# Row maxima of attention scores: one transpose of six columns and three two-head ScalarE operations in place of three transposes and two operations

## Chip, cores and metric

The kernel runs on one core of one Trainium2 chip. The metric is device time in microseconds (us) for one execution of the program. Engines are named as the profile names them: PE (TensorE, matrix products and transposes), PEld (its weight loads), DVE (VectorE), ACT (ScalarE), POOL (GpSimd), SP (SyncE, which issues most DMAs).

## What is computed

The reference is a clustered attention followed by a mixture of experts. Attention has 4 batches, 8 heads, 768 positions and 64 channels. Each query and key is assigned to one of 16 centroids, and a query sees only keys of its own centroid:

```python
mask = q_assign[:, :, :, None] == k_assign[:, :, None, :]
scores = scale * np.matmul(q, k.transpose(0, 1, 3, 2))
scores = np.where(mask, scores, -1000000000.0)
scores = scores - np.max(scores, axis=-1, keepdims=True)
attn = np.exp(scores)
attn = attn / (np.sum(attn, axis=-1, keepdims=True) + 1e-09)
return np.matmul(attn, v).astype(np.float32)
```

The 3072 attention rows of 512 channels then pass one of 8 experts each (two layers, 512 to 1024 to 512, with a relu between them), if a skip score is positive:

```python
e_idx = np.argmax(logits, axis=1)
for e in range(E):
    mask = e_idx == e
    h = np.maximum(xc[mask] @ w1[e], 0.0)
    y[mask] = gate_w[mask, None] * (h @ w2[e])
out[do_compute] = xc + y
```

## The kernel before

The 32 heads are worked on as 16 pairs, numbered 0 to 15. A pair has 24 score steps: two halves of 384 queries (`hf`), six blocks of 128 keys (`kt`), two heads (`a`). One step (`score`) makes a 128x384 tile of transposed scores with two products (L604 and L605), ACT exponentiates it into a slot of the tile PT (L607), and POOL adds the slots up over the key blocks (L613, L619), which gives the denominators. Every six steps a burst of 12 products with v follows (`avs`, L630).

The row maximum is subtracted inside the product. The left operand of L604 holds, below 64 channels and 32 mask rows, rows of constants for each head (a tile of KB); the right operand (a tile of QM, one per head, both in the big tile D) holds the negated maxima of the queries there. So the maxima, which come out of DVE with queries along the partitions, have to be turned into rows:

- `smax` makes scores with queries along the partitions (L569) and DVE reduces them over keys (L571) into a tile M.
- `mneg` (L578, DVE) reduces M to one maximum for each query and head. For a half these are three blocks of 128 queries by two heads, written as columns 96 and 97 of three 128x128 blocks of a tile MX, one MX for each half.
- `mrows` turns each block on PE (L586, three transposes into one PSUM bank, block b at columns 128 b), so that rows 96 and 97 of the bank hold the maxima of the two heads. Two ACT operations (L591), one for each head, then write rows 96 and 97, negated, of QM.

Every instruction of attention is recorded by one planner, `steps`: a heap of tasks with due times in score steps (the table PLAN, with exceptions for pairs 0 to 3 in FIRST). `mrows` of a pair's first half is due 4.5 steps before its first score, and that of its second half 5.5 steps after it. PSUM tiles come from a ring of seven banks: `take` pops the bank that has been free longest, `give` appends one, both at the time when the planner records them. Other users of this ring, which the text below names, are the turned similarities to centroids (L514, read by `first_max` on DVE in L494 and L497, which then gives the bank back), the turned denominators (L678) and the turned attention output of the pair before (L729).

`operand_buffers` runs at the start, before the first pair. On POOL it fills the constant rows of three KB buffers for each head (L289 to L293, 12 fills) and clears the two MX tiles (L297). Behind these, POOL makes the low parts of pair 0's operands (L463, two operations), those of pair 1 (L431, two), clears rows of QM (L405), and then takes up its sums.

Of the kernel before, what the change touches and what calls it, by code (L numbers as in the profile page):

```python
# [13 lines left out]
F32 = mybir.dt.float32  # L14
# [4 lines left out]
AF = mybir.ActivationFunctionType  # L19
ALU = mybir.AluOpType  # L20
AX = mybir.AxisListType
PSUM = bass.MemoryType.PSUM

P = 128
H, S, D, NCL = 8, 768, 64, 16
HP = H // 2
HALF = S // 2
NB = HALF // P
KT = S // P
NS = 2 * 2 * KT  # L30
BIG = 2.0 ** 33

# [47 lines left out]
class Kernel:  # L80
# [167 lines left out]
    def buffers(self):  # L248

        D, both, last = self.D, self.both, self.nbatch * HP - 1  # L250
        assert last % 2 == 1 and last % 3 == 0
        part = lambda at, n, w: [D[:, at + w * j:at + w * (j + 1)] for j in range(n)]
        ops = [part(at, 4, S) for at in (13824, 0, 3072)]
        self.QM, self.KB = [o[:2] for o in ops], [o[2:] for o in ops]
        self.HI = part(6144, 2, S)
        self.QC = [part(at, 4, S) for at in (7680, 10752)]
        raw = both.tile([P, 2, 2, S], F32, name="raw", tag="raw")
        self.RAW = [raw[:, n] for n in range(2)]
        vt = both.tile([P, 2, KT, P], F32, name="vt", tag="vt")
        self.VT = [self.fix.tile([P, KT, P], F32, name="vt0"), vt[:, 0], vt[:, 1]]  # L260
        self.OT = [self.fix.tile([P, S], F32, name=f"oT{n}") for n in range(5)]

        w = part(0, 3, 1024) + [None] * 3 + [D[:, 6144:7168], D[:, 3072:4096]]
        w += part(4096, 2, 1024) + [D[:, 7168:8192], None] + part(8192, 2, 1024) + part(10752, 2, 1024)
        self.W = {"w1h": w[:4], "w1l": w[4:8], "w2h": w[8:12], "w2l": w[12:]}
        self.HT = [u.rearrange("p (f t) -> p f t", t=P) for u in part(13824, 2, 1024)]
        self.X1 = [u.rearrange("p (k t) -> p k t", t=P) for u in part(15872, 2, DM)]
        t = self.PT.rearrange("p n q -> p (n q)")
        self.HS, self.YE, self.XG0 = t[:, :FF], t[:, FF:FF + DM], t[:, FF + DM:FF + 2 * DM]
        self.XO = t[:OT, FF + 2 * DM:FF + 3 * DM]  # L270
# [9 lines left out]
    def operand_buffers(self):  # L280

        nc, fix, npair = self.nc, self.fix, self.npair
        for i in range(min(3, npair)):
            for a in range(2):
                kk = self.KB[i][a].bitcast(F32)

                lo = 64 if i else 96
                if a:
                    nc.gpsimd.memset(kk[96:98, :], 1.0)  # L289
                    nc.gpsimd.memset(kk[lo:97, :], 0.0)  # L290
                else:
                    nc.gpsimd.memset(kk[lo:98, :], 0.0)
                    nc.gpsimd.memset(kk[96:97, :], 1.0)  # L293

        self.MX = [fix.tile([P, NB, P], F32, name=f"MX{hf}") for hf in range(2)]
        for t in self.MX:
            nc.gpsimd.memset(t, 0.0)  # L297

        self.M = [fix.tile([P, KT, 2, 3], F32, name=f"M{n}") for n in range(2)]
        for t in self.M:  # L300
            nc.vector.memset(t[:, :, :, 2:], -BIG / 2)
        nc.vector.memset(self.PT[:, :, HALF:], GUARD / S)
# [24 lines left out]
    def tasks(self, i):  # L327
# [27 lines left out]
        for hf in range(2):  # L355
            add(p["mneg"][hf], self.mneg, hf)
            add(p["mrows"][hf][0], self.mrows, hf, *p["mrows"][hf][1:])
            for g in range(0, KT, GROUP):
                add(12 * hf + 2 * (g + GROUP) + p["av"], self.avs, hf, range(g, g + GROUP))
# [204 lines left out]
    def smax(self, i, n):  # L564
# [8 lines left out]
        if i == 0 and n in range(*WARM[:2]):  # L573
            self.keep_busy(1, WARM[2])

    def mneg(self, i, hf):

        self.nc.vector.tensor_reduce(out=self.MX[hf][:, :, 96:98], in_=self.st[i]["m"][:, hf * NB:(hf + 1) * NB],  # L578
                                     axis=AX.X, op=ALU.max)

    def mrows(self, i, hf, wait, step):

        c, nc = self.st[i], self.nc
        mp = self.take(("MX", i, hf), [P, HALF])
        for b in range(NB):
            nc.tensor.transpose(out=mp[:, b * P:(b + 1) * P], in_=self.MX[hf][:, b, :], identity=self.ident)  # L586
        yield wait
        for a in range(2):
            if a:
                yield step  # L590
            nc.scalar.activation(out=c["qm"][a][96:98, hf * HALF:(hf + 1) * HALF], in_=mp[96:98, :], func=AF.Copy,  # L591
                                 scale=-1.0)
        self.give(("MX", i, hf))

    def pt(self, i, s):
        return self.PT[:, (i * NS + s) % self.NPT, :]

    def score(self, i, s):

        c, nc = self.st[i], self.nc  # L600
        hf, kt, a = s // (2 * KT), s // 2 % KT, s % 2
        sl, ks = slice(hf * HALF, (hf + 1) * HALF), slice(kt * P, (kt + 1) * P)
        ps = self.take("ps", [P, HALF])
        nc.tensor.matmul(ps, lhsT=c["kb"][a][0:98, ks], rhs=c["qm"][a][0:98, sl], start=True, stop=False)  # L604
        nc.tensor.matmul(ps, lhsT=c["kc"][a][:, ks], rhs=c["qc"][a][:, sl], start=False, stop=True)  # L605
        pt = self.pt(i, s)[:, :HALF]
        nc.scalar.activation(out=pt, in_=ps, func=AF.Exp, scale=D ** -0.5)  # L607
# [888 lines left out]
```

## Time and profile before

| | |
|---|---|
| median of 3 runs | 662.63 us (661.48 to 662.72) |
| the profiled execution, its own time | 662.12 us |
| its span, first to last instruction | 660.4 us |
| mean granted clock of PE | 0.989 |
| PE busy | 639.8 us, 97% of the span |
| DVE busy | 505.6 us, 77% |
| ACT busy | 417.3 us, 63% |
| POOL busy | 359.9 us, 54% |

The span is what the profile covers; 1.72 us of the execution's own time lie around it. Attention takes the first 440 us or so, the experts the rest. A busy share is an average over stages with different limits, so each stage has to be looked at by itself.

### The profile page before, as it was taken

What the parts mean: (1) busy time and instruction counts of PE and PEld (TensorE: products, weight loads), DVE (VectorE), ACT (ScalarE), POOL (GpSimd) and SP (SyncE); (2) the same over time, 40 slices, a digit from 0 to 9 for tenths busy, and PEclk for the clock granted to TensorE, in tenths of its full rate; (3) what the DMA queues carried; (4) which work ended last, traced back from release to release, by engine and by line L of the source; (5) the groups of instructions that cost most, each with busy time, mean ns of one, the idle gap of its engine ahead of it and who ended that gap; (6) DMA issues with size and microseconds to landing.
All of it is one profiled execution on the core that took longest, in us unless ns stands there. A gap on an engine that the chain in (4) does not pass through costs nothing.

```text
span 660.4 us, 12489 instructions
## 1 busy us (share of the span) xinstructions
PE 639.8 (97%) x4019; PEld 475.9 (72%) x4019; DVE 505.6 (77%) x1031; ACT 417.3 (63%) x935; POOL 359.9 (54%) x384
## 2 busy tenths in 40 slices
PE   7899999999999999999999999799999999999994
PEld 3667776776767767767767767455798898899893
DVE  7877787688988869998769899786689867666721
ACT  7467778677777777767777778454365454544620
POOL 8876777857758867668677777440331321121101
PEclk9899999999999999999999999799999999999998
DMA  7388647866786466555754652140386758566620
GB/s 216 108 198 223 157 140 197 224 184 171 200 224 175 124 168 163 165 137 158 202 145 119 156 136 82 45 151 25 128 283 222 258 189 276 184 199 226 200 77 33
DMA packets 54323, 110.12 MB, mean 167 GB/s; under 512 B 8599, under 2 KB 22807, under 8 KB 54256
## 3 DMA queue, kind: packets, MB, share of 16 engines
q1 hardware_dynamic: 51232, 101.92, 53.7%
q0 software_dynamic: 2624, 7.18, 3.1%
q8 instruction: 33, 0.54, 0.3%
q14 instruction: 34, 0.28, 0.2%
q10 hardware_dynamic: 400, 0.20, 0.1%
HBM read 60.93 MB, written 10.55 MB: 108 GB/s over the span
## 4 chain that ended last, share of the span: by engine, by line
PE 79%; DVE 8%; issue 6%; DMA 5%; ACT 0%; POOL 0%; POOLq 0%; DVEq 0%
PE ps L630 20%; PE ps L604 11%; PE ps L569 10%; PE ps L605 9%; DMA out<-yo,idw 3%; DVE M L571 3%; PE ph L1030 3%; PE ph L1029 3%; PE ph L1028 3%; PE py L1029 2%; PE py L1028 2%; PE py L1030 2%; PE ps L729 2%; PE ps L586 2%; PE ps L480 2%
## 5 line engine op out<-in xcount | busy, mean ns | idle before, releaser
L619 POOL TENSOR_TENSOR acc<-acc,PT 128x384 f32<-128x384 f32 x246 | 241.6, 1010 | 56.5 <-ACT PT L607 56.1
L607 ACT ACTIVATE PT<-ps 128x384 f32<-128x384 f32 x384 | 184.2, 492 | 94.7 <-PE ps L605 77.8
L571 DVE TENSOR_REDUCE M<-ps 128x1 f32<-128x384 f32 x384 | 200.3, 553 | 47.5 <-PE ps L569 46.5
L630 PE MATMUL ps<-PT,vt 128*64 128x385 f32 x768 | 140.2, 500 | 0.1
L604 PE MATMUL ps<-D 98*128 98x384 f32 x384 | 135.5, 353 | 4.1 <-DVE M L571 3.5
L569 PE MATMUL ps<-D 96*128 96x384 f32 x384 | 135.6, 359 | 0.8 <-ACT D L549 0.7
L605 PE MATMUL ps<-D 128*128 128x384 f32 x384 | 131.0, 341 | 0.0
L630 PEld LDWEIGHTS ps<-PT,vt 128*64 128x64 f32 x768 | 49.8, 137 | 57.8 <-issue 52.9
L604 PEld LDWEIGHTS ps<-D 98*128 98x128 f32 x384 | 73.4, 191 | 24.9 <-issue 19.0
L613 POOL TENSOR_TENSOR acc<-PT 128x384 f32<-128x384 f32 x64 | 54.3, 868 | 67.7 <-ACT PT L607 36.1
L569 PEld LDWEIGHTS ps<-D 96*128 96x128 f32 x384 | 73.7, 193 | 20.4 <-ACT x L751 7.2
L1186 POOL DMA_INDIRECT out<-yo,idw x15 | 20.3, 1350 | 114.0 <-DVE yo L1062 103.8
L605 PEld LDWEIGHTS ps<-D 128*128 128x128 f32 x384 | 73.6, 192 | 0.0
L1314 ACT ACTIVATE hh<-ph 128x256 fp32r<-128x256 f32 x56 | 21.4, 383 | 46.4 <-PE ph L1030 46.4
L1315 DVE SCALAR_TENSOR_TENSOR hl<-ph,hh 128x256 fp32r<-128x256 f32 x56 | 23.6, 422 | 33.6 <-ACT hh L1314 33.4
L1286 ACT ACTIVATE D<-wraw 128x1024 fp32r<-128x1024 f32 (+1 forms) x45 | 44.1, 1002 | 6.2 <-PE py L1030 4.7
L1028 PE MATMUL ph<-x2l,D 128*128 128x256 f32 x168 | 47.7, 284 | 0.0
L1029 PE MATMUL ph<-x2h,D 128*128 128x256 f32 x168 | 47.6, 283 | 0.0
L1028 PE MATMUL py<-D,hh 128*128 128x512 f32 x112 | 45.0, 402 | 0.0
L751 ACT ACTIVATE x<-ps,rs 128x64 f32<-128x64 f32 x162 | 36.1, 322 | 10.1 <-DVE rs L683 9.1
L1287 DVE TENSOR_TENSOR D<-wraw,D 128x1024 fp32r<-128x1024 f32 (+1 forms) x29 | 34.3, 1183 | 6.2 <-ACT D L1286 5.4
L431 DVE TENSOR_TENSOR raw<-raw,D 128x768 fp32r<-128x768 f32 x28 | 38.3, 1367 | 0.0
(311 smaller groups left out, 1068.9 us busy)
## 6 DMA issues: line engine op xcount, KB each, us to landing
wraw<-w SPq DMA_DIRECT2D x72, 512.0 KB, 4.9
D<-D SPq DMA_DIRECT2D x124, 192.0 KB, 3.4
raw<-qk SPq DMA_DIRECT2D x16, 768.0 KB, 5.6
D<-raw SPq DMA_DIRECT2D x60, 192.0 KB, 4.1
vt<-v SPq DMA_DIRECT2D x16, 384.0 KB, 4.4
out<-x SPq DMA_DIRECT2D x31, 192.0 KB, 3.3
D<-mk SPq DMA_DIRECT2D x120, 24.0 KB, 1.9
out<-yo,idw POOLq DMA_INDIRECT x15, 4.5
```

What stands on the lines that cost most here:

```text
L431: eng.tensor_tensor(out=lo.bitcast(F32R), in0=lo, in1=c[f"hi{t}"].bitcast(F32), op=ALU.subtract)
L569: nc.tensor.matmul(sm, lhsT=c["qm"][a][0:96, j * P:(j + 1) * P], rhs=c["kb"][a][0:96, hf * HALF:(hf + 1) * HALF], start=True, stop=True)
L571: nc.vector.tensor_reduce(out=c["m"][:, j, a, hf:hf + 1], in_=sm, axis=AX.X, op=ALU.max)
L604: nc.tensor.matmul(ps, lhsT=c["kb"][a][0:98, ks], rhs=c["qm"][a][0:98, sl], start=True, stop=False)
L605: nc.tensor.matmul(ps, lhsT=c["kc"][a][:, ks], rhs=c["qc"][a][:, sl], start=False, stop=True)
L607: nc.scalar.activation(out=pt, in_=ps, func=AF.Exp, scale=D ** -0.5)
L613: nc.gpsimd.tensor_tensor(out=acc, in0=self.pt(i, s - 2)[:, :HALF], in1=pt, op=ALU.add)
L619: (nc.vector if dve else nc.gpsimd).tensor_tensor(out=acc, in0=acc, in1=pt, op=ALU.add)
L630: nc.tensor.matmul(av[a * D:(a + 1) * D, :], lhsT=c["vt"][:, kt, a * D:(a + 1) * D], rhs=self.pt(i, hf * 2 * KT + kt * 2 + a), start=(kt = ...
L1028: mm(ps, lhsT=ah, rhs=bl, start=first, stop=False)
L1029: mm(ps, lhsT=ah, rhs=bh, start=False, stop=False)
L1286: nc.scalar.activation(out=h[:, cs], in_=r[:, cs], func=AF.Copy)
```

## The change

In all pairs but the first and the last (14 pairs, 28 halves), `mneg` writes the six maxima of a query row (two heads by three blocks) into six neighbouring columns, 96 to 101, of one 128x128 tile. One transpose turns them, so that the bank's rows 96 to 101 hold three blocks of head 0 and three of head 1, all in the same 128 columns. Three ACT operations follow, one for each block b of 128 queries: each reads the six rows, multiplies every row with its own entry of a small constant tile `blocks` (1 in the two rows of block b, 0 in the four others), and writes the result, six rows by 128 columns, for both heads at once. So QM has six maximum rows, of which two are not zero in any column, and KB has six constant rows, -1 in the three rows of its own head and 0 in the others; L604 contracts over 102 rows where it had 98. The bank is given back at the time of the first ACT operation, 0.05 steps earlier than before.

The first and the last pair (`apart`) keep three transposes and two ACT operations, with six rows each, from two tiles MX3 of their own. At the start POOL has 16 fills of constant rows and clears four tiles, and DVE makes `blocks`.

```diff
-                lo = 64 if i else 96
-                if a:
-                    nc.gpsimd.memset(kk[96:98, :], 1.0)
-                    nc.gpsimd.memset(kk[lo:97, :], 0.0)
-                else:
-                    nc.gpsimd.memset(kk[lo:98, :], 0.0)
-                    nc.gpsimd.memset(kk[96:97, :], 1.0)
-
-        self.MX = [fix.tile([P, NB, P], F32, name=f"MX{hf}") for hf in range(2)]
-        for t in self.MX:
+                nc.gpsimd.memset(kk[96:MR, :], -1.0 if a else 0.0)
+                nc.gpsimd.memset(kk[96:96 + NB, :], 0.0 if a else -1.0)
+                if i:
+                    nc.gpsimd.memset(kk[64:96, :], 0.0)
+
+        self.MX = [fix.tile([P, P], F32, name=f"MX{hf}") for hf in range(2)]
+        self.MX3 = [fix.tile([P, NB * (P + 1)], F32, name=f"MX3{hf}") for hf in range(2)]
+        for t in self.MX3 + self.MX:
             nc.gpsimd.memset(t, 0.0)
...
+    def apart(self, i):
+        return i in (0, self.npair - 1)
+
     def mneg(self, i, hf):
 
-        self.nc.vector.tensor_reduce(out=self.MX[hf][:, :, 96:98], in_=self.st[i]["m"][:, hf * NB:(hf + 1) * NB],
-                                     axis=AX.X, op=ALU.max)
+        if self.apart(i):
+            mx = self.MX3[hf].rearrange("p (b c) -> p b c", b=NB)[:, :, 96:MR:NB]
+        else:
+            mx = self.MX[hf][:, 96:MR].rearrange("p (a b) -> p b a", a=2)
+        self.nc.vector.tensor_reduce(out=mx, in_=self.st[i]["m"][:, hf * NB:(hf + 1) * NB], axis=AX.X, op=ALU.max)
...
-        for b in range(NB):
-            nc.tensor.transpose(out=mp[:, b * P:(b + 1) * P], in_=self.MX[hf][:, b, :], identity=self.ident)
+        for b in range(NB if apart else 1):
+            nc.tensor.transpose(out=mp[:, b * P:(b + 1) * P],
+                                in_=self.MX3[hf][:, b * P:(b + 1) * P] if apart else self.MX[hf], identity=self.ident)
         yield wait
-        for a in range(2):
-            if a:
-                yield step
-            nc.scalar.activation(out=c["qm"][a][96:98, hf * HALF:(hf + 1) * HALF], in_=mp[96:98, :], func=AF.Copy,
-                                 scale=-1.0)
+        if apart:
+            for a in range(2):
+                if a:
+                    yield step
+                nc.scalar.activation(out=c["qm"][a][96:MR, n0:n0 + HALF], in_=mp[96:MR, :], func=AF.Copy)
+        else:
+            rows = self.QM2[i % 3][96:MR]
+            for b in range(NB):
+                nc.scalar.activation(out=rows[:, :, n0 + b * P:n0 + (b + 1) * P],
+                                     in_=mp[96:MR, :P].unsqueeze(1).to_broadcast([MR - 96, 2, P]), func=AF.Copy,
+                                     scale=self.blocks[96:MR, b:b + 1])
         self.give(("MX", i, hf))
...
-        nc.tensor.matmul(ps, lhsT=c["kb"][a][0:98, ks], rhs=c["qm"][a][0:98, sl], start=True, stop=False)
+        nc.tensor.matmul(ps, lhsT=c["kb"][a][:MR, ks], rhs=c["qm"][a][:MR, sl], start=True, stop=False)
```

Three places show what this does to the order of instructions. In these rows a bank of the ring is ps0_81 to ps6_87, ident_101 is the identity, and "waits" names the engines whose semaphores an instruction waits for. Line numbers of the changed kernel are its own (L586 has become L595, L514 L516, L678 L694, L729 L745, L630 L646, L569 L571).

The first place is PE at the second half of pair 3. Before, the maxima (L586), the turned similarities (L514), the turned denominators (L678) and the turned output of the pair before (L729):

```order
L586 MATMUL ps6_87<-ident_101,MX1_196 128x128 [waits DVE_49,Activation_49]
L586 MATMUL ps6_87<-ident_101,MX1_196 128x128 x2
L514 MATMUL ps4_85<-ident_101,ss_1197 128x128 [waits DVE_49,Activation_49]
L514 MATMUL ps4_85<-ident_101,ss_1197 128x128 x2
...
L678 MATMUL ps3_84<-ident_101,sr_1204 128x128 [waits Activation_49]
L678 MATMUL ps3_84<-ident_101,sr_1204 128x128 x2
L729 MATMUL ps4_85<-ident_101,oT2_96 128x128 [waits DVE_49]
L729 MATMUL ps4_85<-ident_101,oT2_96 128x128 x2
L630 MATMUL ps7_88<-PT_65,vt0_93 64x385 x6
L569 MATMUL ps6_87<-D_64 128x384 [waits Activation_49]
```

The same place in the changed kernel:

```order
L595 MATMUL ps3_84<-ident_101,MX1_202 128x128 [waits DVE_49,Activation_49]
L516 MATMUL ps4_85<-ident_101,ss_1202 128x128 [waits DVE_49,Activation_49]
L516 MATMUL ps4_85<-ident_101,ss_1202 128x128 x2
...
L694 MATMUL ps2_83<-ident_101,sr_1209 128x128 [waits Activation_49]
L694 MATMUL ps2_83<-ident_101,sr_1209 128x128 x2
L745 MATMUL ps3_84<-ident_101,oT2_96 128x128 [waits Activation_49]
L745 MATMUL ps3_84<-ident_101,oT2_96 128x128 x2
L646 MATMUL ps7_88<-PT_65,vt0_93 64x385 [waits DVE_49]
L646 MATMUL ps7_88<-PT_65,vt0_93 64x385 x5
L571 MATMUL ps4_85<-D_64 128x384 [waits DVE_49]
```

Two transposes are gone, and the banks have changed places: the turned output took the bank of the similarities (ps4_85, which DVE gives back) and now takes that of the maxima (ps3_84, which ACT gives back), and the next L569 the other way round.

The second place is ACT at the same half of pair 3: the denominators (L669), the maxima and two exponentials (L607). Before:

```order
L487 ACTIVATE ss<-ps_83 128x384 [waits PE_49]
L669 ACTIVATE sr<-ps_81 128x384 [waits DVE_49,PE_49]
L591 ACTIVATE D<-ps_87 2x384 [waits DVE_49,PE_49]
L591 ACTIVATE D<-ps_87 2x384
L607 ACTIVATE PT<-ps_86 128x384 [waits PE_49,Pool_49]
L607 ACTIVATE PT<-ps_83 128x384 [waits PE_49,Pool_49]
```

In the changed kernel:

```order
L489 ACTIVATE ss<-ps_87 128x384 [waits PE_49]
L685 ACTIVATE sr<-ps_81 128x384 [waits DVE_49,PE_49]
L606 ACTIVATE D<-ps_83,blocks 6x2x128 [waits PE_49]
L606 ACTIVATE D<-ps_83,blocks 6x2x128 x2
L623 ACTIVATE PT<-ps_86 128x384 [waits PE_49,Pool_49]
L623 ACTIVATE PT<-ps_87 128x384 [waits PE_49,Pool_49]
```

The two operations have become three, at the same place in ACT's queue, and the exponentials stand behind them as before.

The third place is POOL at the start, from the fills for pair 2's buffers on. Before:

```order
L292 MEMSET D 34x768
L293 MEMSET D 1x768 [waits Pool_49]
L289 MEMSET D 2x768
L290 MEMSET D 33x768 [waits Pool_49]
L297 MEMSET MX_195 128x384 [waits Pool_49]
L297 MEMSET MX_196 128x384
L463 TENSOR_TENSOR D<-raw,D 64x768 [waits DMAHW5_49,DMAHW1_49,DVE_49]
L463 TENSOR_TENSOR D<-raw,D 64x768 [waits DMAHW6_49,Pool_49]
L431 TENSOR_TENSOR raw<-raw,D 128x768 [waits PE_49,DMAHW2_49,Activation_49,Pool_49]
L431 TENSOR_TENSOR raw<-raw,D 128x768 [waits PE_49,Activation_49]
```

In the changed kernel:

```order
L291 MEMSET D 6x768
L292 MEMSET D 3x768 [waits Pool_49]
L294 MEMSET D 32x768
L299 MEMSET MX_203 128x387 [waits Pool_49]
L299 MEMSET MX_204 128x387
L299 MEMSET MX_201 128x128
L299 MEMSET MX_202 128x128
L465 TENSOR_TENSOR D<-raw,D 64x768 [waits DMAHW5_49,DMAHW1_49,DVE_49]
L465 TENSOR_TENSOR D<-raw,D 64x768 [waits DMAHW6_49,Pool_49]
L433 TENSOR_TENSOR raw<-raw,D 128x768 [waits PE_49,DMAHW2_49,Activation_49,Pool_49]
L433 TENSOR_TENSOR raw<-raw,D 128x768 [waits PE_49,Activation_49]
```

Four more fills of constant rows (of which the last three rows of 16 are shown) and two more cleared tiles stand ahead of the low parts of pairs 0 and 1.

## Rows read from the trace of the kernel before

**Rows 1.** The page: part 1, and the chain that ended last, by engine (part 4).
```profile
PE 639.8 (97%) x4019; PEld 475.9 (72%) x4019; DVE 505.6 (77%) x1031; ACT 417.3 (63%) x935; POOL 359.9 (54%) x384
...
PE 79%; DVE 8%; issue 6%; DMA 5%; ACT 0%; POOL 0%; POOLq 0%; DVEq 0%
```

**Rows 2.** Busy us by window: start:end, length, PE, PEld, DVE, ACT, POOL, PEclk, DMA, GB/s.
```profile
22.00:24.00 2.00, 1.98 (x9) 1.58 (x8) 1.91 (x5) 1.22 (x3) 1.92 (x4) 0.50 0.04 8
100.00:125.00 25.00, 25.00 (x155) 17.55 (x154) 18.31 (x36) 18.93 (x47) 18.87 (x20) 1.00 0.72 199
```

**Rows 3.** PE's waits: line, who was waited for, us in total, times, longest us.
```profile
PE ps L604 <- DVE M L571: 3.5, 1, 3.5
...
PE ps L729 <- DVE eqc L497: 0.6, 2, 0.3
```

**Rows 4.** Timeline of PE, second half of pair 3: start us, us, line, op.
```profile
106.01 0.55 PE L586 MATMUL ps<-ident,MX 128*128 128x128 f32 x3
...
108.12 0.55 PE L729 MATMUL ps<-ident,oT 128*128 128x128 f32 x3
```

**Rows 5.** Timeline of PE, first half of pair 4, in a wide and a narrow window.
```profile
119.64 0.34 PE L569 MATMUL ps<-D 96*128 96x384 f32 x1
119.82 0.49 PE L586 MATMUL ps<-ident,MX 128*128 128x128 f32 x3
120.24 0.55 PE L630 MATMUL ps<-PT,vt 128*64 128x385 f32 x2
...
119.82 0.27 PE L586 MATMUL ps<-ident,MX 128*128 128x128 f32 x1
```

**Rows 6.** Timeline of PE where no transpose stands between L569 and L630.
```profile
40.05 0.33 PE L569 MATMUL ps<-D 96*128 96x384 f32 x1
40.45 0.87 PE L630 MATMUL ps<-PT,vt 128*64 128x385 f32 x4
```

**Rows 7.** Timeline of ACT: the maxima, and operations with a scale in a tile.
```profile
14.37 1.02 ACT L549 ACTIVATE D<-ps,sel 32x384 fp32r<-32x384 f32 x2
...
106.74 0.86 ACT L591 ACTIVATE D<-ps 2x384 fp32r<-2x384 f32 x2
...
109.19 1.33 ACT L751 ACTIVATE x<-ps,rs 128x64 f32<-128x64 f32 x6 [0.65 <-DVE rs L683]
```

**Rows 8.** Timeline of POOL at the start.
```profile
3.00 0.73 POOL L292 MEMSET D<- 2x768 f32 x1
...
12.20 0.78 POOL L297 MEMSET MX<- 128x384 f32 x2
13.41 3.71 POOL L463 TENSOR_TENSOR D<-raw,D 64x768 fp32r<-64x768 f32 x2 [0.43 <-DVE D L463]
17.20 3.57 POOL L431 TENSOR_TENSOR raw<-raw,D 128x768 fp32r<-128x768 f32 x2
```

**Rows 9.** Timeline of PE and DVE at the first score and pair 1's centroids.
```profile
20.52 0.45 PE L604 MATMUL ps<-D 98*128 98x384 f32 x1 [0.57 <-ACT D L591]
...
20.43 0.75 DVE L502 TENSOR_TENSOR eqc<-eqc,wts 128x384 f32<-128x384 f32 x1
21.81 0.56 DVE L507 TENSOR_TENSOR oh<-wts,mwc 128x384 bf16<-128x384 f32 x1
...
22.42 0.24 PEld L527 LDWEIGHTS <-oh 128*128 128x128 bf16 x3 [0.53 <-DVE oh L507]
```

**Rows 10.** Timeline of DVE and POOL where both work from SBUF.
```profile
9.63 0.56 DVE L502 TENSOR_TENSOR eqc<-eqc,wts 128x384 f32<-128x384 f32 x1
...
42.43 1.22 DVE L502 TENSOR_TENSOR eqc<-eqc,wts 128x384 f32<-128x384 f32 x1
...
410.61 6.75 DVE L989 TENSOR_TENSOR cc<-ohd,ecode 128x48 f32<-128x48 bf16 x1
...
39.86 8.53 POOL L619 TENSOR_TENSOR acc<-acc,PT 128x384 f32<-128x384 f32 x8
...
410.13 7.16 POOL L619 TENSOR_TENSOR acc<-acc,PT 128x384 f32<-128x384 f32 x8
```

More of the change, by code (lines that the diff above doesn't have):

```diff
@@ L29 @@
 KT = S // P
+MR = 96 + 2 * NB
 NS = 2 * 2 * KT
@@ L253, in buffers @@
         ops = [part(at, 4, S) for at in (13824, 0, 3072)]
+        self.QM2 = [D[:, at:at + 2 * S].rearrange("p (a s) -> p a s", a=2) for at in (13824, 0, 3072)]
         self.QM, self.KB = [o[:2] for o in ops], [o[2:] for o in ops]
@@ L282, in operand_buffers @@
         nc, fix, npair = self.nc, self.fix, self.npair
+        self.blocks = fix.tile([P, NB], F32, name="blocks")
+        nc.vector.tensor_tensor(out=self.blocks, in0=self.ident[:, 96:96 + NB], in1=self.ident[:, 96 + NB:MR], op=ALU.add)
         for i in range(min(3, npair)):
@@ L574, in smax @@
             self.keep_busy(1, WARM[2])
+    def apart(self, i):
+        return i in (0, self.npair - 1)
     def mneg(self, i, hf):
-        self.nc.vector.tensor_reduce(out=self.MX[hf][:, :, 96:98], in_=self.st[i]["m"][:, hf * NB:(hf + 1) * NB],
-                                     axis=AX.X, op=ALU.max)
+        if self.apart(i):
[3 more added lines that the diff above has]
+        self.nc.vector.tensor_reduce(out=mx, in_=self.st[i]["m"][:, hf * NB:(hf + 1) * NB], axis=AX.X, op=ALU.max)
     def mrows(self, i, hf, wait, step):
         c, nc = self.st[i], self.nc
+        n0, apart = hf * HALF, self.apart(i)
         mp = self.take(("MX", i, hf), [P, HALF])
-        for b in range(NB):
-            nc.tensor.transpose(out=mp[:, b * P:(b + 1) * P], in_=self.MX[hf][:, b, :], identity=self.ident)
+        for b in range(NB if apart else 1):
+            nc.tensor.transpose(out=mp[:, b * P:(b + 1) * P],
+                                in_=self.MX3[hf][:, b * P:(b + 1) * P] if apart else self.MX[hf], identity=self.ident)
         yield wait
-        for a in range(2):
-            if a:
-                yield step
-            nc.scalar.activation(out=c["qm"][a][96:98, hf * HALF:(hf + 1) * HALF], in_=mp[96:98, :], func=AF.Copy,
-                                 scale=-1.0)
+        if apart:
[9 more added lines that the diff above has]
+                                     scale=self.blocks[96:MR, b:b + 1])
         self.give(("MX", i, hf))
```

## The prediction, made before the changed kernel was run

> **What bounds the kernel now.** I read the page first. PE is busy for 97% of the span, and the chain of work that ended last runs through PE for 79% of it [rows 1]. That is an average, so the next view is the table of busy time by window: in a stretch of pairs 3 and 4 PE is busy for 25.00 of 25 us at a granted clock of 1.00, while DVE (18.3) and ACT (18.9) have six us left [rows 2]. The list of PE's waits then has only one of weight inside attention, 3.5 us for one DVE reduction near the end, and two of 0.3 us each for L497 [rows 3]. So between the start and about 400 us PE's own instructions set the pace, and a PE instruction that is taken out there is worth the time until the next one can start.
>
> **What is removed.** 14 pairs times 2 halves times 2 transposes: 56 of PE's instructions. One is drawn 0.27 us long, but they overlap: in the narrow window one takes 0.27, in the wide one three take 0.49, so they start (0.49 - 0.27) / 2 = 0.11 us apart [rows 5]. Two fewer are worth 0.22 us, where the next instruction follows at once. That holds at a second half, where another three transposes (L514) come next. At a first half L630 comes next, and there I check it against a place without transposes: from L569 to L630 it takes 0.40 us with nothing between [rows 6] and 0.60 with three transposes [rows 5], so no more than 0.20 can be won. The term is 14 x 0.22 + 14 x 0.20 = 5.9 us. It can't be much more; it is less where PE then waits for something else.
>
> **What ACT gains.** Two operations on 2x384 take 0.86 us together; three on 6x2x128, 256 elements in a row and each with its scale read from a tile, take their place. No row shows this shape. The nearest from below is L751, 64 elements with a scale from a tile, 1.33 / 6 = 0.22 us each; from above L549, 384 elements with such a scale, 1.02 / 2 = 0.51 [rows 7]. So three cost between 0.67 and 1.53 us. By the number of elements, 0.22 + 0.29 x 192/320 = 0.40 each and 1.18 for the three, which I take: 0.32 us more in each half, 9 us in all on an engine with a quarter of its time left. Who waits for it? Behind them stand two exponentials, and behind those ACT is idle for 0.65 us before L751 [rows 7]; the first scores that read the maxima are four steps away by their due times. That covers 0.3 us.
>
> What is not covered is the bank. At the second half of a pair the turned output of the pair before, L729, used to take the bank that L497 on DVE gives back; now it takes the bank of the maxima, free when the third ACT operation ends. L729 stands at 108.12, 1.38 us after the ACT operations start at 106.74 [rows 4, 7]. With the transposes gone PE is there 0.22 earlier, after 1.16 us, and ACT needs 1.18 and a few hundredths for the signal: a wait of about 0.05. Nine of the second halves have this distance, within 0.06 us: 0.4 us in all. At the lower bound the wait is nothing, at the upper one 1.53 - 1.16 = 0.37, 3.3 us in all. In exchange the two waits for L497 go: 0.6 us won [rows 3].
>
> Here the Trainium skill speaks against the change. "ScalarE: Activation LUTs", section "What ACT_TABLE_LOAD costs", prices an operation at 186 ns plus 0.833 ns an element, 93 ns more for a scale read from a tile, with about 93 ns overlap between neighbours; as an estimate from that page three would take 1.29 us, and the sum would come out about 1 us higher. The trace agrees on the cost of the scale only in part: L549's pair lies above L591's by 0.08 us for each operation [rows 7].
>
> **What moves at the start.** POOL makes 12 fills and two cleared tiles from 3.00 to 12.98 before it is ready for L463, which starts at 13.41 and waits for DVE [rows 8]. The fills start (12.20 - 3.00) / 12 = 0.77 us apart, whatever their number of rows. Now there are 16, so the tiles start at about 3.00 + 12.3 = 15.3 at that pitch, or 14.7 if the fills without a wait of their own go closer; with 0.8 for the two larger tiles and 0.3 for the two smaller (a third of 0.39 each, rounded up), L463 starts at about 16.0 and ends at 19.7, some 2.5 us late. Its first reader, the second head's first score, comes behind the first L604 at 20.52 [rows 9], so that is hidden. L431 is next: it ran from 17.20 to 20.77 [rows 8] and would run from 19.7 to 23.3.
>
> That puts L431 on top of two DVE operations which read two operands from SBUF, L502 at 20.43 and L507 at 21.81; PE's L527 waits for L507 [rows 9]. Such operations get longer beside POOL's sums: L502 takes 0.56 us beside POOL's fills and 1.22 in the middle of eight POOL sums [rows 10]. So I let each wait for the POOL operation that is running. L431's two operations of 1.8 us end at about 21.5 and, after L502 has been let in, at 23.7. L502 then ends at 21.9, L505 follows, L507 waits from 22.5 to 23.7 and ends at 24.15, where it ended at 22.37: 1.8 us. PE waits behind L527 and works at half clock there (0.50, the 1.2 GHz level, [rows 2]) without a gap until the bursts begin, so 1.8 us stay. The bounds: nothing, if DVE gets its turn first, and 2.4 us if DVE has to wait for both of L431's operations.
>
> "SBUF — State Buffer" of the Trainium skill, section "Who interferes with whom", has the same: a DVE instruction with two SBUF inputs blocks against a POOL instruction that reads SBUF, and not against one that only writes. The trace shows it, 1.22 against 0.56 us [rows 10].
>
> The other edits cost nothing. `blocks` is one small DVE operation at about 6 us, where DVE next waits for PE; if it didn't, it would be some 0.1 us. The four longer fills cost what the shorter ones do. L604 over 102 rows instead of 98: L605 over 128 runs at the same pace. DVE's L578 writes as many elements. The DMA of pair 2's input, which waits for L463, goes out 2.5 us later, and its reader, the similarities of pair 2, is due five score steps behind the first score; the mask rows' DMAs wait for L405 behind L431, but also for the mask that follows L527, so they shift with it.
>
> **The sum,** against the profiled execution's own time: 662.12 - 5.9 (transposes) + 0.4 (bank) - 0.6 (waits for L497) + 1.8 (start) = 657.8 us. That execution lies 0.5 us below the median and inside the three runs' spread, so I leave the sum where it is: **657.8 us**.
>
> **Rivals.**
>
> 1. The start costs nothing: L431 leaves the gaps that DVE needs, or POOL is ready earlier. For it: L463 had 0.43 us in hand at the start of its run [rows 8]. Against: the fills' pitch is steady. 662.1 - 6.1 = 656.0 us.
> 2. ACT is at the upper bound, and L729 waits 0.37 us at each of nine pairs: 657.8 + 2.9 = 660.7. For it: no row has this shape, which writes two places from one. Against: it moves a third less for each operation than L549.
> 3. Slower than before: a DVE operation is caught behind a whole run of POOL sums. It happens once already: L989, 48 elements a row, takes 6.75 us, until the POOL run from 410.13 to 417.29 ends [rows 10], and PE then waits 3.5 us. By the rule of one instruction it would be 1 us. If one more operation on which PE waits is caught so, 657.8 + 6.7 = 664.5; it decides from 4.3 us on, that is, five sums of 0.9 us. For it: the change shifts PE and ACT against each other by half a us in every pair. Against: elsewhere in these rows one add was the longest wait.
> 4. The mirror of it: L989 falls outside the run, PE's 3.5 us wait goes: 654.3. As the order there is the same on all engines, I give it little.
> 5. The change takes nothing off PE's path: PE waits for others as long as it is early (L630 for exponentials, L569 for banks). Then only the start is left: 662.1 + 1.8 = 663.9. Against it stands a PE that is busy for 25.00 of 25 us.
>
> The same SBUF page says, in its section "SBUF: two separate sides", that the one who starts first holds the port for one whole instruction; by that, L989 should have waited for one sum, and the trace does not agree.
>
> **How the numbers follow.** Forecast 0.52 (its own range 656.6 to 659.2), rival 1 0.22, rival 2 0.08, rival 3 0.06, rival 4 0.07, rival 5 0.05. A measurement of this kernel can tell about 0.2%, 1.3 us, from no change: faster is below 661.3, slower above 664.0. Faster: the forecast, 1, 4 and half of 2 (the upper bound with a late start ends near 661), 0.85. Slower: 3 and part of 5, 0.08. The rest, 0.07, is no change. The range reaches from 655.2 to 661.2: it takes in rivals 1 and 2 and leaves out 3, 4 and 5, 0.18.
>
> **What would show it.** In the profile after: 40 transposes for the maxima (28, and 12 in the first and the last pair) where there were 96; one transpose of 0.27 us where three took 0.49; three ACT operations in 1.1 to 1.3 us; L729 (now L745) with small waits for ACT; L463 and L431 on POOL 2.5 us later, L507 longer or later, and L527 near 24.2. The bursts of L630 should come some 0.4 us earlier for each pair gone by, less what the start costs. It would be wrong if PE showed new waits for banks of some tenths in every pair, if PE's half clock at the start lasted longer with the wait, or if the DVE operation near 410 were gone or had a twin.

## The result, and the profile after

The changed kernel takes 653.13 us (median of 6 runs, 652.87 to 654.12); beside it the kernel before took 661.92 (6 runs, 659.60 to 662.72). The ratio is 0.9877, 95% interval 0.9857 to 0.9897: 8.8 us faster. Forecast were 657.8 us, in a range from 655.2 to 661.2. The direction was right and the time fell below the range.

The page of the changed kernel: its span, part 1, and the chain that ended last by engine (part 4).

```profile
span 651.5 us, 12396 instructions
...
PE 632.2 (97%) x3963; PEld 468.3 (72%) x3963; DVE 507.7 (78%) x1032; ACT 426.6 (65%) x963; POOL 364.1 (56%) x390
...
PE 75%; DMA 8%; DVE 8%; issue 7%; POOL 0%; ACT 0%; POOLq 0%; SPq 0%; DVEq 0%
```

Against [rows 1], PE has 56 instructions less, the two transposes in 28 halves, and ACT 28 more, one in each of these halves. PE is 7.6 us less busy, and the span is 8.9 us shorter. Where the rest comes from these sums don't say. For that I line up the two traces by the exponentials on ACT (L607, now L623), which come in the same order in both, and read the start of the first one of a half. Three points cut the span into four stretches:

| | to pair 0, step 12 | to pair 14, step 12 | to pair 15, step 12 | to the end | span |
|---|---|---|---|---|---|
| before | 33.98 | 369.83 | 32.20 | 224.39 | 660.4 |
| changed | 36.62 | 364.53 | 25.59 | 224.76 | 651.5 |
| difference | +2.64 | -5.30 | -6.61 | +0.37 | -8.9 |

So the shorter pairs gave 5.30 us and the start took 2.64. Together that is 2.7 us of gain. The other 6.6 us come out of one stretch near 410 us, in which the numbers of transposes and of ACT operations are those of before.

The start, on POOL (start us, us, line, operation):

```profile
14.60 0.73 POOL L294 MEMSET D<- 32x768 f32 x1
15.39 1.08 POOL L299 MEMSET MX<- 128x387 f32 x4
16.55 3.68 POOL L465 TENSOR_TENSOR D<-raw,D 64x768 fp32r<-64x768 f32 x2
20.31 3.90 POOL L433 TENSOR_TENSOR raw<-raw,D 128x768 fp32r<-128x768 f32 x2
```

on DVE, which works beside it:

```profile
20.40 2.15 DVE L504 TENSOR_TENSOR eqc<-eqc,wts 128x384 f32<-128x384 f32 x1
22.58 0.55 DVE L507 TENSOR_REDUCE mwc<-eqc 128x24 f32<-128x384 f32 x1
23.17 1.45 DVE L509 TENSOR_TENSOR oh<-wts,mwc 128x384 bf16<-128x384 f32 x1
```

and PE, which waits for it:

```profile
24.68 0.50 PE L529 MATMUL ps<-ident_bf,oh 128*128 128x128 bf16 x3 [2.12 <-DVE oh L509]
```

Against [rows 8, 9]: POOL's low parts stand 3.1 us later, the two DVE operations with two operands in SBUF fall on L433 and take 2.15 and 1.45 us where they took 0.75 and 0.56, and PE's L529 starts 2.26 us later. Behind it PE works at half clock, as these windows have it (start:end, length, busy us of PE, PEld, DVE, ACT and POOL, PEclk, DMA, GB/s):

```profile
24.00:26.00 2.00, 1.32 (x6) 1.32 (x7) 1.91 (x4) 0.67 (x1) 1.94 (x4) 0.50 0.04 11
26.00:28.00 2.00, 2.00 (x8) 2.00 (x8) 1.34 (x4) 0.93 (x2) 1.92 (x4) 0.50 0.09 22
```

In the pairs, the maxima on ACT and the turned output on PE at the second half of pair 3:

```profile
108.47 1.19 ACT L606 ACTIVATE D<-ps,blocks 6x256 fp32r<-6x256 f32 x3
```

```profile
107.74 0.33 PE L595 MATMUL ps<-ident,MX 128*128 128x128 f32 x1
...
109.71 0.55 PE L745 MATMUL ps<-ident,oT 128*128 128x128 f32 x3
```

The three operations take 1.19 us, and L745 starts 0.05 us behind their end. The group of L606 names who waited for it (its count, ns of one as min, median and max, and then us and times):

```profile
L606 ACT ACTIVATE D<-ps,blocks x84: 451/452/469, 45.5 to 395.2; 6x256 fp32r<-6x256 f32 x84
...
  PEld ps L745: 1.3, 8
```

Near 410 us, DVE and POOL:

```profile
407.93 3.20 DVE L1005 TENSOR_TENSOR cc<-ohd,ecode 128x48 f32<-128x48 bf16 x1
411.17 0.20 DVE L1008 TENSOR_REDUCE c<-cc 128x6 f32<-128x48 f32 x1
```

```profile
407.45 7.19 POOL L635 TENSOR_TENSOR acc<-acc,PT 128x384 f32<-128x384 f32 x8
```

and the windows around it, with the same columns:

```profile
409.00:412.00 3.00, 3.00 (x19) 2.19 (x13) 2.97 (x4) 1.99 (x6) 3.00 (x4) 1.00 0.00 0
412.00:415.00 3.00, 3.00 (x19) 2.06 (x21) 3.00 (x7) 2.75 (x5) 2.65 (x4) 1.00 0.01 3
415.00:418.00 3.00, 3.00 (x23) 1.95 (x23) 1.74 (x7) 2.29 (x7) 1.19 (x2) 1.00 0.23 72
418.00:421.00 3.00, 3.00 (x26) 1.49 (x19) 2.92 (x4) 2.16 (x6) 1.45 (x2) 1.00 0.42 168
```

This is the operation that took 6.75 us [rows 10], in front of the reductions on which PE waited 3.5 us [rows 3]. It meets the same run of eight sums, begins 0.48 us behind the start of that run's first sum as before, and ends after 3.20 us, 0.07 us behind the end of the fourth sum, while the run goes on to 414.64. PE has no wait here, and its granted clock stays at 1.00.

### The profile page after: what moved, and what is told of

The parts are those of the page before. It is cut to its first block, busy times and chain, and to the rows that moved or that the text cites. A ratio compares the mean times of both kernels' runs of the same rounds, so it can differ in the third digit from the quotient of the medians.

```text
span 651.5 us, 12396 instructions
## 1 busy us (share of the span) xinstructions
PE 632.2 (97%) x3963; PEld 468.3 (72%) x3963; DVE 507.7 (78%) x1032; ACT 426.6 (65%) x963; POOL 364.1 (56%) x390
## 4 chain that ended last, share of the span: by engine, by line
PE 75%; DMA 8%; DVE 8%; issue 7%; POOL 0%; ACT 0%; POOLq 0%; SPq 0%; DVEq 0%
PE ps L646 20%; PE ps L620 11%; PE ps L571 10%; PE ps L621 10%; DMA out<-yo,idw 5%; DVE M L573 3%; PE ph L1045 2%; PE ph L1044 2%; PE ph L1046 2%; PE py L1045 2%; PE py L1044 2%; PE ps L745 2%; PE py L1046 2%; PE ps L482 2%; PE ps L682 1%
## 5 line engine op out<-in xcount | busy, mean ns | idle before, releaser
L623 ACT ACTIVATE PT<-ps 128x384 f32<-128x384 f32 x384 | 183.3, 492 | 80.1 <-PE ps L621 56.3
L646 PE MATMUL ps<-PT,vt 128*64 128x385 f32 x768 | 138.4, 495 | 0.1
L571 PE MATMUL ps<-D 96*128 96x384 f32 x384 | 135.5, 359 | 0.9 <-ACT D L551 0.7
L620 PE MATMUL ps<-D 102*128 102x384 f32 x384 | 135.3, 352 | 0.6 <-ACT D L602 0.6
L646 PEld LDWEIGHTS ps<-PT,vt 128*64 128x64 f32 x768 | 49.3, 136 | 58.1 <-issue 51.2
L620 PEld LDWEIGHTS ps<-D 102*128 102x128 f32 x384 | 73.3, 191 | 21.1 <-issue 18.6
L571 PEld LDWEIGHTS ps<-D 96*128 96x128 f32 x384 | 73.5, 192 | 20.8 <-issue 6.6
L433 DVE TENSOR_TENSOR raw<-raw,D 128x768 fp32r<-128x768 f32 x28 | 38.8, 1385 | 0.0
```

Source lines behind the costliest of these rows:

```text
L433: eng.tensor_tensor(out=lo.bitcast(F32R), in0=lo, in1=c[f"hi{t}"].bitcast(F32), op=ALU.subtract)
L571: nc.tensor.matmul(sm, lhsT=c["qm"][a][0:96, j * P:(j + 1) * P], rhs=c["kb"][a][0:96, hf * HALF:(hf + 1) * HALF], start=True, stop=True)
L620: nc.tensor.matmul(ps, lhsT=c["kb"][a][:MR, ks], rhs=c["qm"][a][:MR, sl], start=True, stop=False)
L646: nc.tensor.matmul(av[a * D:(a + 1) * D, :], lhsT=c["vt"][:, kt, a * D:(a + 1) * D], rhs=self.pt(i, hf * 2 * KT + kt * 2 + a), start=(kt = ...
```

## Experiments

Each kernel was timed beside the kernel before on the same chip. Experiments 1 to 4 ran together, so did 5 to 7 with the first of 11, the four of 8, and the rest; the kernel before had medians of 661.06, 660.92, 661.63 and 661.34 us in these four series.

**1. The operation moved out of the run of eight sums, in the kernel before.**

```diff
-         91.67, 91.68, 97.66, 97.67, 97.68, 97.69, 97.7)
+         83.7, 83.71, 97.66, 97.67, 97.68, 97.69, 97.7)
```

> The kernel before, with the operation cc (L989) and the small sum behind it (L992) due eight score steps earlier (83.7 instead of 91.67), in front of the run of POOL sums that held it for 6.75 us. Theory: the last 6.6 us of what the change won come only from L989 no longer being held. Then this kernel wins them without any change to the transposes: no wait of PE near 411 to 418, granted clock 1.00 in the 12 us behind it, about 655.5 us (658.5 if only the 3.5 us wait goes and the low clock stays). Rival: PE would have waited there anyway, for the next DVE operation or for a bank, and the change won these microseconds by its shorter pairs: 661 to 662 us.

Measured 654.24 us, ratio 0.9894 (0.9876 to 0.9913). The operation stands at 402 us now:

```profile
402.03 0.74 DVE L989 TENSOR_TENSOR cc<-ohd,ecode 128x48 f32<-128x48 bf16 x1
```

It has not left POOL's sums altogether: it starts in the second of a run of four, and ends 0.07 us behind that second sum.

```profile
400.87 3.62 POOL L619 TENSOR_TENSOR acc<-acc,PT 128x384 f32<-128x384 f32 x4 [1.73 <-ACT PT L607]
```

The stretch between pair 14 and pair 15 takes 25.38 us, where it took 32.20; the pairs before it are 369.82 us long, as they were. So that one operation cost the kernel before 6.8 us at its old place, which is more than the transposes are worth (5.3). The rival, that PE would have waited there anyway, has fallen.

**2. Only the four fills and two tiles more, in the kernel before.**

```diff
                     nc.gpsimd.memset(kk[96:97, :], 1.0)
+                if i:
+                    nc.gpsimd.memset(kk[64:96, :], 0.0)
...
-        for t in self.MX:
+        spare = [fix.tile([P, P], F32, name=f"MXS{hf}") for hf in range(2)]
+        for t in self.MX + spare:
```

> The kernel before, with four more fills of constant rows (rows 64 to 95 of the buffers of pairs 1 and 2, written twice) and two more small cleared tiles on POOL at the start, nothing else. Theory: POOL's low parts of pair 0 and of pair 1 come about 3 us later, DVE's L502 and L507 fall on them, L527 starts some 2.2 us later and the pairs run 2.3 to 2.7 us late: 664.5 us if L989 is held as before, 658 if the shift alone sets it free. Rival: the late start of the changed kernel has to do with its six rows or its order on PE, not with POOL: 662 us.

Measured 664.11 us, ratio 1.0045 (1.0029 to 1.0061). Pair 0's step 12 comes at 36.58, 2.60 us late, which is the loss of the changed kernel (2.64) without any of its transposes or rows. The operation cc is held 6.77 us: the later start alone does not set it free.

**3. Twelve fills in the changed kernel.** As the kernel before did, one fill covers rows 64 to 95 along with some of the constant rows.

```diff
-                nc.gpsimd.memset(kk[96:MR, :], -1.0 if a else 0.0)
-                nc.gpsimd.memset(kk[96:96 + NB, :], 0.0 if a else -1.0)
-                if i:
-                    nc.gpsimd.memset(kk[64:96, :], 0.0)
+                lo = 64 if i else 96
+                if a:
+                    nc.gpsimd.memset(kk[96:MR, :], -1.0)
+                    nc.gpsimd.memset(kk[lo:96 + NB, :], 0.0)
+                else:
+                    nc.gpsimd.memset(kk[lo:MR, :], 0.0)
+                    nc.gpsimd.memset(kk[96:96 + NB, :], -1.0)
```

> The changed kernel, with 12 fills of constant rows where it has 16 (the rows 64 to 95 are covered by the fill that writes zeros to rows 96 to 98 or 96 to 101, as the kernel before did it). Theory: POOL is ready 3 us earlier, L509 is back at 0.5 to 0.7 us, L529 starts near 22.6 instead of 24.7: 650.8 us, if L1005 stays as free as it is. Rival: L504 and L509 are slow whatever POOL does, or the gain is lost behind the bursts: 653 us. If L1005 is held again by the shift: 657 us.

Measured 649.95 us, ratio 0.9823 (0.9807 to 0.9840). POOL is back where it was, and DVE with it:

```profile
13.38 3.71 POOL L468 TENSOR_TENSOR D<-raw,D 64x768 fp32r<-64x768 f32 x2
17.17 3.57 POOL L436 TENSOR_TENSOR raw<-raw,D 128x768 fp32r<-128x768 f32 x2
```

```profile
20.39 0.77 DVE L507 TENSOR_TENSOR eqc<-eqc,wts 128x384 f32<-128x384 f32 x1
21.19 0.55 DVE L510 TENSOR_REDUCE mwc<-eqc 128x24 f32<-128x384 f32 x1
21.78 0.56 DVE L512 TENSOR_TENSOR oh<-wts,mwc 128x384 bf16<-128x384 f32 x1
```

Pair 0's step 12 comes at 33.87, 2.75 us sooner than in the changed kernel, and nothing of it is given back. The four fills were the whole loss at the start.

**4. Three transposes and two ACT operations in all pairs of the changed kernel.**

```diff
-        return i in (0, self.npair - 1)
+        return True
```

> The changed kernel with three transposes and two ACT operations in all pairs, as it has them in the first and the last (six rows, 16 fills and the late start stay). Theory: the one transpose is worth 5.3 us over pairs 1 to 14, and what happens to L1005 near 410 us is a matter of when it meets the POOL run, not of the transposes: 658.4 us if it is free, 665 if it is held. Rival 1: the six rows and the tiles, not the number of transposes, made the pairs faster: 653 us. Rival 2: the transposes bring nothing and all the gain is that of L1005: 653 us too, with pairs that keep their distance from the kernel before at 2.65 us late throughout.

Measured 658.43 us, ratio 0.9959 (0.9943 to 0.9974), 5.30 us above the changed kernel, which was timed in another series, in which the kernel before stood 0.9 us higher. In the traces the stretch of the pairs is 369.80 us long, that of the kernel before; so the one transpose with its three operations is worth 5.27 us, and the six rows and the tiles nothing. The operation cc is held for 3.19 us here too, with three transposes: its freedom doesn't come from them.

**5. Where do the tiles lie?** The changed kernel and the runs of experiments 3 and 4 were free, the kernel before and that with more fills held, and in all five cc began at the same distance from POOL's sums to 0.01 us. Left was what the changed kernel moves without an instruction: its larger MX tiles and `blocks` put every later tile in SBUF 1120 bytes farther.

```diff
+        self.gap = fix.tile([P, 280], F32, name="gap")
         for t in self.MX:
```

> The kernel before, with an unused tile of 1120 bytes a partition behind the MX tiles, so that every later tile of SBUF (M, the sums acc, ohd, cc) lies at the very address that it has in the changed kernel; no instruction is added. The operation cc was held 6.75 us in the kernel before and with more fills, and 3.20 us in the changed kernel and its two variants, although it met the POOL sums at the same phase to 0.01 us in all five. Theory of the address: where acc, ohd and cc lie decides how long it is held. Then 3.20 us here and no wait of PE: 655.0 us. Rival, the timing: ACT's operations around it come 0.03 us later in the changed kernel, or something else in its program does it. Then it is held 6.75 us and the time is that of the kernel before, 661 to 662 us.

Measured 655.81 us (6 runs, 654.84 to 657.22), ratio 0.9928 (0.9912 to 0.9943), with the instructions of the kernel before. The operation, and the windows of 6 us from there on:

```profile
409.46 3.20 DVE L990 TENSOR_TENSOR cc<-ohd,ecode 128x48 f32<-128x48 bf16 x1
```

```profile
412.00:418.00 6.00, 6.00 (x35) 4.25 (x34) 5.97 (x15) 4.92 (x9) 4.16 (x5) 1.00 0.07 21
418.00:424.00 6.00, 6.00 (x46) 3.62 (x46) 3.78 (x9) 5.14 (x14) 2.87 (x4) 1.00 0.32 103
```

**6. The same with 32 bytes** (`[P, 8]` in that line).

> The kernel before, with an unused tile of 32 bytes a partition behind the MX tiles. 1120 bytes are 17.5 times 64; the additional tiles of the run with more fills were 1024 bytes, 16 times 64, and changed nothing. If the address theory holds and only the place within 64 bytes counts: 3.20 us for cc and 655.0 us. If the distance itself counts: 6.75 us and 661 to 662 us, while the shift by 1120 bytes wins. If timing is the cause: 661 to 662 us in both.

Measured 661.10 us, ratio 1.0004 (0.9993 to 1.0015). Held:

```profile
410.64 6.76 DVE L990 TENSOR_TENSOR cc<-ohd,ecode 128x48 f32<-128x48 bf16 x1
```

```profile
412.00:418.00 6.00, 2.66 (x16) 2.07 (x12) 5.97 (x3) 2.06 (x5) 5.33 (x6) 0.99 0.00 0
418.00:424.00 6.00, 5.84 (x19) 3.67 (x21) 4.85 (x14) 2.87 (x4) 0.00 (x0) 0.50 0.12 36
```

Beside the windows of the run above these show both halves of the price. PE does nothing for 3.3 us, and then works for 6 us at half clock (0.50, the 1.2 GHz level), where the free kernel does 46 instructions in the time of 19.

**7. 32 bytes in the changed kernel** (the same line in front of the loop over its MX tiles).

> The changed kernel, with an unused tile of 32 bytes behind its MX tiles, so that acc, ohd and cc lie within 64 bytes as they do in the kernel before. Theory of the address within 64 bytes: cc is held 6.75 us again, PE waits 3.5 us near 411, the low clock follows: 653.1 + 6.6 = 659.7 us, which is what the change is worth without it (5.3 us of transposes less 2.65 us of start). Rivals (timing, or the distance): 653.1 us.

Measured 659.33 us, ratio 0.9970 (0.9958 to 0.9983): an unused tile of 32 bytes a partition takes 6.2 us of the change's 8.8 away. The operation and PE's longest wait:

```profile
409.11 6.77 DVE L1006 TENSOR_TENSOR cc<-ohd,ecode 128x48 f32<-128x48 bf16 x1
```

```profile
PE ps L621 <- DVE M L574: 3.5, 1, 3.5
```

It is what the change does when nothing comes free at 410 us, and it lies in the forecast range. With runs 6 and 7 the place within 64 bytes has fallen as a rule: by it, 32 bytes would have freed the one and not only caught the other.

**8. Whose place?** Four kernels with the instructions of the kernel before, which move groups of tiles apart from each other: the routing tiles (ohd, cc) by 1120 bytes; acc and the other tiles of attention by 1120 and the routing tiles by 1152; cc alone by 1120; ohd by 1120 and cc by 1152. Each edit is an unused tile, as above, in front of the named one.

> The kernel before, with the unused tile of 1120 bytes in front of the routing tiles alone: ohd and cc lie where the changed kernel has them, acc (POOL's sums) stays where it was. If the operands of the held operation decide (its own address), cc is free after 3.20 us and the time is 655 to 656 us. If the place of acc decides: held 6.75 us, 661 us.

> The opposite: acc and all tiles of attention lie where the changed kernel has them, the routing tiles 32 bytes farther (ohd and cc are 1152 bytes from their old place). If the place of acc decides: free, 655 to 656 us. If that of ohd or cc decides: held, 661 us. If both have to fit, this one and the last are held.

> The kernel before, with only the tile cc (the output of the held operation) and the small tiles behind it 1120 bytes farther, cc then beginning where it does in the changed kernel, at a multiple of 4096 bytes. If the address of the output decides: free, 655 to 656 us. If not: held, 661 us.

> The kernel before, with ohd (the input of the held operation) 1120 bytes farther, as in the changed kernel, and cc 1152 bytes farther, 32 off from it. If the address of the input decides: free, 655 to 656 us. If not: held, 661 us.

Ratios: 0.9917 (0.9894 to 0.9939), 0.9969 (0.9931 to 1.0006), 0.9991 (0.9976 to 1.0006), 0.9952 (0.9919 to 0.9984). The single times say more than these:

| moved | runs near 655 us | runs near 661 us | cc in the profiled run |
|---|---|---|---|
| routing tiles 1120 | 9 (654.5 to 655.7) | 1 (661.4) | 3.20 us |
| attention 1120, routing 1152 | 4 (654.3 to 654.8) | 6 (660.7 to 662.7) | 3.20 us |
| cc 1120 | 0 | 10 (659.7 to 662.2) | 6.77 us |
| ohd 1120, cc 1152 | 5 (654.7 to 655.8) | 5 (659.7 to 662.3) | 6.80 us |

Each expectation named one tile whose place would decide, and no such tile fits all four. One and the same program runs either way, some 6 us apart, and none of these 40 runs lies between 656 and 659. The cc column is from the profiled run alone, and it agrees with that run's time in all four. So the place of the tiles doesn't decide it; it moves the odds, from none of ten to nine of ten. (These 40 runs are from one chip, those of experiments 1 to 7 from another, where the odds need not be the same.) Of the kernel before none of 94 runs took less than 659.4 us, and of the changed kernel none of six more than 654.2.

One rival is not excluded. Just behind the start of the first of the eight sums, ACT starts an exponential. In the six profiles where cc was held at its due place this is 0.05 to 0.06 us behind, in the kernel before 0.055; in six of the seven where it was free there it is 0.075 to 0.09, and experiment 5 is one of these, with no instruction changed. So in most of the free profiles ACT, and PE with it, stands some 0.03 us later against the sums. That is not needed, as the seventh, the second row of the table, was free at 0.054; whether it is a cause or a companion no run tells.

**9. The operation one reduction later and one sooner,** in the kernel before, so at another phase in the same run of sums (92.67 and 90.67 in the line of experiment 1).

> The kernel before, with cc one score step later, that is, behind one more reduction L571 of 0.46 us, in the same run of POOL sums; all tiles lie where they did. Theory of the phase: at another phase against the sums it can be let in at the end of any of them, so it is likely held for a shorter time than the rest of the run, and the time falls by up to 6.6 us, to 655 us; if it is held to the end of the run again, 6.3 us from a start 0.46 us later, the time is 661 us. Theory of the tiles' places: they are the same, so it is held to the end of the run, 661 us.

> The same with cc one reduction sooner, 0.46 us, in front of the sum that began 0.48 us before it in the kernel before, so near the end of the sum before that. Theory of the phase: it is let in sooner, 655 us, or else held for 7.2 us to the end of the run, 661.5 us. Theory of the places: held to the end, 661.5 us.

Measured 660.55 us, ratio 0.9985 (0.9971 to 0.9998), and 660.38, ratio 0.9988 (0.9974 to 1.0002). One reduction later it starts at 412.41, as the L571 ahead of it waits 2.39 us for PE, and it ends behind POOL's last sum, which ends at 416.18; sooner, it starts at 409.01:

```profile
412.41 3.84 DVE L989 TENSOR_TENSOR cc<-ohd,ecode 128x48 f32<-128x48 bf16 x1
```

```profile
409.01 6.25 DVE L989 TENSOR_TENSOR cc<-ohd,ecode 128x48 f32<-128x48 bf16 x1
```

It is held to the end of the run in both, and PE waits 3.0 and 3.2 us. So neither of the two new phases frees it, as the theory of the phase had it. With the tiles of the kernel before it was held to the end of this run of sums at all three starts. That is no rule for every run: in the kernel before the same operation, also among POOL sums without a pause, took 0.87 us at 202 and at 308 us, to 0.07 us behind the one sum that was running.

**10. The bank given back as before,** in the changed kernel, and in the best version.

```diff
+        if not apart:
+            yield step
         self.give(("MX", i, hf))
```

> The changed kernel, with the bank of the maxima given back 0.05 steps later, as the kernel before did it. The bank order is then that of before: L745's eight waits of 0.16 us for L606 go (1.3 us) and two of 0.3 us for the operation eqc return (0.6 us). Theory: 653.1 - 0.7 = 652.4 us, with pairs that gain 0.16 us more each at nine second halves. Rival: what L745 waits for is work that PE would wait for a moment later anyway: 653.1 us, with no step at these halves. If cc is held again by the shift, 659 us.

Measured 653.29 us, ratio 0.9876 (0.9855 to 0.9897). The pairs take 364.93 us, 0.40 more than in the changed kernel. L745 no longer waits for L606, but for DVE:

```profile
PE ps L747 <- DVE eqc L499: 1.1, 2, 0.5
```

Seen half by half, second halves get 0.02 to 0.07 us shorter where a wait of 0.16 us is gone, as most of it was covered; those of pairs 6 and 10 get 0.34 and 0.36 us longer. Between pairs 2 and 6 halves change by up to 0.35 us either way, which about cancels. The earlier give is worth 0.40 us in these traces, and the expectation had the wrong sign; by the medians, 653.29 and 653.13, it can't be seen.

**11. The best version: 12 fills, and cc at 83.7,** and with it the bank given back later.

> The changed kernel with 12 fills (649.95 us) and with cc due at 83.7. Theory: cc is taken out of the run of sums for good, but in this kernel it cost PE nothing even there (3.20 us held, no wait of PE): 649.5 to 650.0 us. Moving it in the kernel before won more than the wait and the low clock, 0.3 us by which the later phases moved; if that is a gain of its own, 649.3 us. Rival: the earlier place delays slotacc's users and the gather behind them: 650.5 to 651 us.

> The changed kernel with 12 fills, with cc at 83.7 (649.26 us) and with the bank given back later. Theory: 0.7 us less, 648.6 us. Rival: 649.3 us.

Measured 649.26 us, ratio 0.9830 (0.9814 to 0.9847), and 649.74, ratio 0.9826 (0.9807 to 0.9845). The first of them beats the changed kernel by 3.9 us. In the three profiles with cc at 83.7 it took 0.74 us, and none of the 14 runs of these kernels has the 5 to 7 us more of a held one; that this holds wherever tiles lie was not run. Its stretch to pair 15 takes 25.42 us, 0.17 less than that of the changed kernel. With the later give the pairs take 364.88 us where they took 364.36, so the earlier give wins 0.5 us here too. By time the first can't be told apart from the 649.95 of experiment 3.

## Why the prediction was wrong

Step by step, in its own order:

- **What bounds the kernel**: right. PE's own instructions set the pace, and the pairs' stretch is the same to 0.1 us in all kernels with three transposes (369.75 to 369.85).
- **The transposes**: 5.9 us won here and 0.2 by the banks made 6.1; measured 5.30 against the kernel before and 5.27 against experiment 4. Somewhat too large. A first half gains 0.18 us, where 0.20 was the bound and the value taken.
- **ACT**: right. Three operations take 1.19 us (1.18 forecast). The estimate from the Trainium skill's page "ScalarE: Activation LUTs", section "What ACT_TABLE_LOAD costs", 1.29 us, was 0.10 too high here.
- **The bank**: eight waits of 0.16 us, not nine of 0.05. But a wait of PE's weight load is not its price; experiment 10 has the balance at -0.40 us, forecast were +0.4 and -0.6.
- **The start**: right in every link, and undersized: 2.64 us for 1.8. L465 was 0.5 us later than forecast (16.55 for 16.0); by the forecast's own pitch of the fills the sum is 15.3 + 1.1 for the tiles = 16.4, and 16.0 was taken, between this and closer fills. L509 waited for L433's end, with 1.45 us. Of the 2.64 us, 2.26 are the delay of L529; the rest comes behind it, where PE works at the low level until 28 us. Between the medians of experiment 2 the late start costs 3.05 us.
- **L989**: the step that failed. The sum took PE's 3.5 us wait as given, as the order of instructions around it stays what it was. With the same order and the same start, 0.48 us into the run of sums, the operation took 3.20 us instead of 6.75, the wait was gone, and the stretch to pair 15 fell from 32.20 to 25.59 us. The wait is decided by something that the order does not show. Rival 4 was nearest and got 0.07, though not by its own way: it had L989 outside the run, where it was let in halfway through it.
- **The price of rival 4** was also short: it counted the wait of 3.5 us and not the half clock behind it. Together they are 6.6 us, so that the rival should have stood at 651.2. With a start of 2.64 and 5.30 for the pairs it gives 662.12 + 2.64 - 5.30 - 6.61 + 0.37 = 653.22 (the 0.37 is the last stretch), and the changed kernel's profiled execution took 653.23. This sum has to close, as its terms are read from these two executions; that the three large terms have the causes named here is what experiments 1 to 5 show. The 6.6 us are not fixed either: in the six profiles that were held at the due place the stretch took 30.71 to 32.23 us, 5.1 to 6.6 above the 25.59 of the free ones.

Without the operation's release the change is worth what experiment 7 shows, 659.3 us against 660.9, and 653.1 with it. That a shift of the tiles is enough to release it is shown (experiment 5 does it with no other edit), and so is that a shift catches it again (experiment 7); by which way the shift acts is not. What decides in one execution, at the end of the fourth sum, whether DVE is let in, stays open. It is not the address within 64 bytes alone, nor the phase as far as two other phases tell, and the same program did both.

## What to carry to other kernels

A wait in the trace of before that ends with another engine's run of work, as cc's did with POOL's sums, can go or come with an edit that doesn't touch it, here one that only moves addresses. Count it as a term with two values, with the clock's fall behind it in the price, and not as a part of the baseline. If a kernel has one, take it out first: two numbers in a table were worth 6.8 us here, more than the transposes, and the next measurement is then easier to read. And an edit that adds work on an engine off PE's path at the start has to be followed to the operation that it delays, not to the first one that hides it.

## What the hardware showed that was not expected

- A DVE operation that needs 0.21 us at most (the first kernel of experiment 9 shows this at 202.55 us) took 6.2 to 6.8 us behind seven or eight POOL sums that leave no time between them, and at another time was let in after four of them. The Trainium skill's page "SBUF — State Buffer", section "SBUF: two separate sides", lets the first one keep the port for one whole instruction; neither of these agrees with that, while the 0.74 us of experiment 1 and the 0.87 us at 202 us in the kernel before, each to the end of one sum, do.
- Which of the two it is can differ between executions of one program. Moving tiles by 32 to 1152 bytes changed the share of free runs, from none of ten to nine of ten.
- At the start, the same instructions meet different clocks in different executions. In the profiled run of the kernel before, the granted clock was 0.50 from 22 to 24 us [rows 2], in that of experiment 1 it was 1.00, and pair 0's step 12 came 1.14 us sooner:

```profile
22.00:24.00 2.00, 1.80 (x13) 1.49 (x12) 2.00 (x5) 1.66 (x4) 1.92 (x4) 1.00 0.03 8
```

It is a part of the spread of the kernel before (659.4 to 663.7 us), whose runs below 660 us in the four series had a mean granted clock of 0.994 or 0.995 and those above 662 us 0.988 to 0.990. It is also the reason why experiments 1 and 5 won 0.6 and 0.7 us more in their profiles than in the stretch near 410 us.
